# Four tiles instead of six transposed on TensorE, first norms of ten tiles moved behind all statistics, half of w3 loaded in phase one

## The chip, the core and the metric

The kernel runs on one core of one Trainium2 chip. The metric is the device time of one launch in microseconds (us); lower is better. The times before the change are six runs with a median of 1507.94 us (1507.79 to 1508.09). The engines are named as the profile names them: PE is TensorE (matmul), PEld its weight loads, DVE is VectorE, ACT is ScalarE, POOL is GpSimd, SP is SyncE, which here only starts DMA transfers. A trailing q (SPq, POOLq) marks the issuing side of a queue.

## What is computed

The input `x` has 2048 tokens of 1024 bf16 numbers. It is normalized to `xn`; the output is `x` plus a memory-augmented attention over `xn` plus an MLP-mixer block over `xn`. The change lies in the first part of the mixer block:

```python
xn = layernorm(x)
# mixer block, with x := xn
h  = gelu(layernorm(xn) @ w1)                   # phase one
hs = shifted(h, by quarter of the columns) @ w2 # phase two
x1 = xn + hs
B  = x1 + gelu(layernorm(x1) @ w3) @ w4         # phase three, w3 is 1024 x 3584
out = x + attention(xn) + B
```

Both layer norms of phase one have the same row statistics as source: the second norm of `x` is computed straight from `x` with a scale of its own, so one set of statistics gives the "first norm" (`xn`, needed in phase two and in the attention) and the "second norm" (`xn2`, the operand of the product with w1).

## The kernel before

The 2048 tokens are 16 tiles of 128 rows. Weights are k-major: a tile of 128 rows times 1024 columns is 8 blocks of 128 x 128.

**Phase one.** For tile n, `norm_stats` makes the statistics: two BN statistics instructions on DVE (L266, L269), an aggregation (L270), one small DVE instruction that writes `ab` (L271) and a power on POOL that turns it into the scales `rr` (L273). From tile 8 on POOL also makes a negated product `nm2` (L275). `norm2` writes `xn2`: on DVE for tiles 0 to 7 (L282), on ACT for tiles 8 to 15 (L284). The product with w1 needs `xn2` transposed, in `xn2T`, which holds two tiles. Tiles below `NPE` are transposed by TensorE, eight 128 x 128 products with the identity (L303), and copied out of PSUM by ACT (L304). The others are transposed by one DMA from SP (L286). `norm1` writes `xn` into `xn_keep` (L292, DVE).

`stage1(n0, nt, ...)` (L319) is one pass over w1 for `nt` tiles: eight groups, one for each 128 output columns, of eight matmuls (L324) with 128 x nt moving columns. ACT reads each group out of PSUM with a gelu (L326) into `hTB`. Four PSUM buffers take turns, so a group waits for the gelu of the group four before it. `between` hangs further work behind the gelu of one of the eight groups. Tile 0 has a pass of its own (`stage1_k`), tiles 1, 2 and 3 have one each; tiles 4 and 5, 6 and 7 and so on share a pass with 256 columns. I call the passes by their tiles: pass 3, pass 4+5.

Engines run their instructions in the order in which the program gives them, and this part of the order is written by hand on all engines. `prep(n)` (L386) issues the second norm of tile n, the statistics of tile n+1 and the first norm of tile n-2, four tiles ahead of the pass. Tiles of `x` stand in ten buffers (`xt`), so the load of tile n+10 waits for the first norm of tile n. SP issues its DMAs one by one: loads of `x`, transposes, w2 in two halves (L253), four stores of `xn` to a scratch (L407), then parts of w3 (L210). `load_w3` takes the next part of two k-rows and half the columns, 896 KB; four parts make the left half of w3. In the kernel before, two parts are issued at the end of phase one and one each behind tiles 3 and 7 of phase two (L436). The right half is issued at the start of phase three in two DMAs of 1792 KB (L446).

**Phase two** (L414 to L437): for each tile 16 matmuls of 512 columns (L421), an addition of `xn_keep` and statistics on DVE, a norm on ACT (L433), a DMA transpose from SP into `xn3T` (L434) and a store of `x1` issued by POOL (L435). **Phase three** starts with L550 (w3, left half first) and L576 (w4). The value, attention and output phases follow (L607, L673, L731).

Of the kernel before, what the change touches and what calls it, by code (L numbers as in the profile page):

```python
# [16 lines left out]
F32 = mybir.dt.float32  # L17
# [6 lines left out]
P = 128  # L24
S = 2048
D = 1024
KT = D // P
NT = S // P
# [49 lines left out]
def kernel(  # L78
# [112 lines left out]
    with tc.manual_schedule(engines={mybir.EngineType.PE, mybir.EngineType.SP, mybir.EngineType.Pool}), ExitStack() as actx:  # L191
# [6 lines left out]
        with ExitStack() as bctx:  # L198
# [13 lines left out]
            with ExitStack() as hctx:  # L212
# [7 lines left out]
                with ExitStack() as p0:  # L220
                    big = p0.enter_context(tc.tile_pool(name="p0big", bufs=1))
                    ring = p0.enter_context(tc.tile_pool(name="p0ring", bufs=3))
                    w1_sb = big.tile([P, KT, D], BF16)
                    NPE = 6

                    xts = {}

                    def load_x(n):
                        if n < NT:
                            xts[n] = ring.tile([P, D], BF16, tag="xt", bufs=10, name=f"xt{n}")  # L230
                            if n == 0:
                                nc.scalar.dma_start(xts[n][:, 512:], x_v[:, n, 512:])
                                nc.sync.dma_start(xts[n][:, :512], x_v[:, n, :512])
                            else:
                                (nc.gpsimd if n == 12 else nc.sync).dma_start(xts[n][:], x_v[:, n, :])

                    m0 = hTB[:M, 0, 16:16 + D]
                    nc.gpsimd.dma_start(m0, A_mem0[0])
# [18 lines left out]
                    def norm_stats(n, part=None):  # L257

                        if n >= NT:
                            return  # L260
                        xt = xts[n]
                        if n not in stats:
                            stats[n] = [ring.tile(shape, F32, tag=tag, bufs=6, name=f"{tag}{n}") for tag, shape in (("st", [P, 2, 6]), ("mv", [P, 2]), ("ab", [P, 2]), ("rr", [P, 2]), ("nm2", [P, 1]))]
                        st, mv, ab, rr, nm2 = stats[n]
                        if part in (None, 0):
                            nc.vector.bn_stats(st[:, 0, :], xt[:, 0:512])  # L266
                        if part == 0:
                            return
                        nc.vector.bn_stats(st[:, 1, :], xt[:, 512:1024])  # L269
                        nc.vector.bn_aggr(mv[:], st[:])  # L270
                        nc.vector.scalar_tensor_tensor(ab[:], epsm[:], mv[:, 1:2], epsa[:], op0=ALU.mult, op1=ALU.add)  # L271
                        for c in (slice(1, 2), slice(0, 1)) if n == 0 else (slice(0, 2),):
                            nc.gpsimd.tensor_tensor(rr[:, c], ab[:, c], neghalf[:, c], op=ALU.pow)  # L273
                        if n >= 8:
                            nc.gpsimd.tensor_scalar(nm2[:], mv[:, 0:1], rr[:, 1:2], -1.0, op0=ALU.mult, op1=ALU.mult)  # L275
# [13 lines left out]
                    def norm1(n):  # L289
                        st, mv, ab, rr, nm2 = stats[n]  # L290
                        xn = xn_keep[n // 4][:, n % 4]
                        nc.vector.tensor_scalar(xn, xts[n][:], mv[:, 0:1], rr[:, 0:1], op0=ALU.subtract, op1=ALU.mult)  # L292
                        if n < 3:
                            load_x(n + 10)
                        return xn

                    def transposes(xn2, xn2T, jj, half, halves=False):
# [21 lines left out]
                    def stage1(n0, nt, xn2T, between, j0=0):  # L319
                        w = nt * P  # L320
                        for co in range(KT):
                            ps = psum.tile([P, 512], F32, tag="mm", bufs=4)
                            for k in range(KT):
                                nc.tensor.matmul(ps[:, :w].rearrange("p (n t) -> p n t", t=P), w1_sb[:, k, co * P:(co + 1) * P],  # L324
                                                 xn2T[:, j0:j0 + nt, k, :], start=(k == 0), stop=(k == KT - 1))
                            nc.scalar.activation(hTB[:, co, 2 + n0 * P:2 + n0 * P + w], ps[:, :w], ACTF.Gelu_apprx_tanh)  # L326
                            for f in between.get(co, ()):
                                f()
# [20 lines left out]
                    def tr(n, half, halves=False):  # L349
                        transposes(xn2s[n], tiles2[n - n % 2], n % 2, half, halves)  # L350
# [12 lines left out]
                    nc.gpsimd.memset(hTB[:, :, S + 2:S + 4], 0.0)  # L363
                    load_consts(4)
                    nc.gpsimd.memset(sums[:], 1.0)
                    for n in range(1, 6):
                        if n > 1:
                            norm_stats(n + 1, 0)
                        norm2_of(n)
                        norm_stats(n + 1, 1 if n > 1 else None)  # L370
                        if n > 1:
                            norm1(n - 2)
                        if n == 1:
                            stage1_k(tiles2[0])
                        elif n < 4:
                            stage1(n - 1, 1, tiles2[(n - 1) // 2 * 2], {6 - n: [lambda n=n: tr(n, 0)], 7 - n: [lambda n=n: tr(n, 1)]}, (n - 1) % 2)

                    def ahead(n):
                        norm_stats(n + 1, 0)
                        norm2_of(n)  # L380
                        norm_stats(n + 1, 1)
                        if n == 6:
                            norm1(n - 2)

                    stage1(3, 1, tiles2[2], {0: [lambda: tr(4, 0)], 2: [lambda: tr(4, 1), lambda: ahead(6)], 4: [lambda: tr(5, 0)], 5: [lambda: tr(5, 1), lambda: ahead(7)]}, 1)
                    def prep(n):  # L386
                        norm2_of(n)
                        norm_stats(n + 1)
                        if n == 8:
                            norm1(n - 3)  # L390
                        norm1(n - 2)

                    for n0 in range(4, NT, 2):
                        between = {c: [] for c in range(KT)}
                        if n0 + 4 < NT:
                            between[1 + 2 * (n0 == 4)] += [lambda n0=n0: prep(n0 + 4)]
                            between[4 + 2 * (n0 == 4)] += [lambda n0=n0: prep(n0 + 5)]
                        stage1(n0, 2, tiles2[n0], between)
                        if n0 == 4:
                            for n in range(13, NT):  # L400
                                load_x(n)
                        elif n0 in (6, 10):
                            load_w2(n0 // 10)
                    for n in (NT - 2, NT - 1):
                        norm1(n)
                    for i in range(4):
                        nc.sync.dma_start(xn_v[:, 4 * i:4 * i + 4, :], xn_keep[i][:])  # L407
                    for i in range(2):
# [3 lines left out]
                with ExitStack() as p2:  # L412
                    ring = p2.enter_context(tc.tile_pool(name="p2ring", bufs=4))
                    for n in range(NT):  # L414
                        x1 = ring.tile([P, D], F32, tag="x1")
                        st = ring.tile([P, 2, 6], F32, tag="st")
                        for ch in range(2):
                            ps = psum.tile([P, 512], F32, tag="mm", bufs=4)
                            for k in range(KT):
                                o = 2 + n * P + SH[k]  # L420
                                nc.tensor.matmul(ps[:], hTB[:, k, o:o + P], w2_sb[:, k, ch * 512:(ch + 1) * 512], start=(k == 0), stop=(k == KT - 1))  # L421
                            nc.vector.tensor_tensor(x1[:, ch * 512:(ch + 1) * 512], ps[:], xn_keep[n // 4][:, n % 4, ch * 512:(ch + 1) * 512], op=ALU.add)
                            nc.vector.bn_stats(st[:, ch, :], x1[:, ch * 512:(ch + 1) * 512])
                        mv = ring.tile([P, 2], F32, tag="mv")
                        nc.vector.bn_aggr(mv[:], st[:])
                        a = ring.tile([P, 1], F32, tag="a")
                        nc.vector.tensor_scalar(a[:], mv[:, 1:2], EPS, None, op0=ALU.add)
                        r3 = ring.tile([P, 1], F32, tag="r3")
                        nc.gpsimd.tensor_tensor(r3[:], a[:], neghalf[:, 0:1], op=ALU.pow)
                        nm3 = ring.tile([P, 1], F32, tag="nm3")  # L430
                        nc.gpsimd.tensor_scalar(nm3[:], mv[:, 0:1], r3[:], -1.0, op0=ALU.mult, op1=ALU.mult)
                        xn3 = ring.tile([P, D], BF16, tag="xn3")
                        nc.scalar.activation(xn3[:], x1[:], ACTF.Identity, bias=nm3[:], scale=r3[:])  # L433
                        nc.sync.dma_start_transpose(xn3T[n // 4][:, n % 4], xn3[:])  # L434
                        nc.gpsimd.dma_start(R1_v[:, n, :], x1[:])  # L435
                        if n in (3, 7):  # L436
                            load_w3()  # L437

            with ExitStack() as p3:
                psum3 = p3.enter_context(tc.tile_pool(name="psum3", bufs=2, space=PSUM))  # L440
# [593 lines left out]
```

## Time and profile before

| what | value |
|---|---|
| median of six runs | 1507.94 us |
| the profiled execution's own time | 1507.74 us |
| its span in the profile | 1506.0 us |
| granted TensorE clock, all stages | 1.00 |
| phase one on PE (first pass to last gelu group) | 7.46 to 66.4 us |
| phase two on PE | 66.4 to 121.7 us |
| PE busy in 24.21 to 66.40 us | 42.12 of 42.19 us |
| PE busy in 66.40 to 121.70 us | 54.98 of 55.30 us |
| DMA busy share, 31 to 67 us / 67 to 121 us | 0.87 / 1.03 |
| DVE busy share, 24 to 31 us / 67 to 121 us | 6.79 of 7.0 us / 46.9 of 54 us |

The rows of the table are the answers of the profile for single stretches of time. "Busy" of PE includes overlapping ends of pipelined matmuls: a matmul row says 219 ns for 128 columns, while the starts of neighbouring ones lie 56 ns apart. For costs on PE the distance of the starts counts, not the row's length. Some matmul records are missing (49 of 50 in each stretch of phase two), which looks like a gap of 0.2 us and is none. The trace also keeps for each DMA the time at which its completion is signalled; "lands" in this text is that time.

### The profile page before, as it was taken

The numbers are of one execution on the slowest core, as the hardware profiler recorded it, in microseconds if no ns is written. First come the engines' busy times: TensorE is split into PE (matmuls) and PEld (weight loads), VectorE is DVE, ScalarE is ACT, GpSimd is POOL, SyncE is SP. The second block draws the span as 40 slices with busy tenths as digits, with TensorE's granted clock in tenths as the row PEclk, the third lists the DMA queues.
The fourth block names the chain that finished last, engine by engine and source line by source line (L and its number), as shares of the span: only waits on it lengthen the run. The fifth ranks groups of instructions, "written<-read, shape, count | busy, mean of one in ns | idle before, by whom it ended". The sixth has DMA issues, their size and how long they took to land.

```text
span 1506.0 us, 24219 instructions
## 1 busy us (share of the span) xinstructions
PE 1496.4 (99%) x9757; PEld 803.2 (53%) x9828; DVE 546.7 (36%) x1148; ACT 501.8 (33%) x1140; POOL 166.2 (11%) x234
## 2 busy tenths in 40 slices
PE   9999999999999999999999999999999999999999
PEld 8744444445454444444466645664665455545555
DVE  8382330100110112221146624651564166516642
ACT  6433103013012011111256614650663266406630
POOL 4141020211211221100000010001000100010001
PEclk9999999999999999999999999999999999999999
DMA  7999762353455777622389956992997299918921
GB/s 191 277 266 327 214 178 89 134 202 113 154 161 139 193 239 253 209 98 84 126 226 252 244 125 174 255 233 78 240 253 203 72 229 225 214 63 204 212 49 51
DMA packets 306194, 272.89 MB, mean 181 GB/s; under 512 B 155766, under 2 KB 272280, under 8 KB 306080
## 3 DMA queue, kind: packets, MB, share of 16 engines
q1 hardware_dynamic: 284704, 193.18, 51.5%
q0 software_dynamic: 20544, 76.89, 15.0%
q8 instruction: 79, 1.29, 0.4%
q10 hardware_dynamic: 832, 1.25, 0.3%
q14 instruction: 35, 0.29, 0.1%
HBM read 190.05 MB, written 45.29 MB: 156 GB/s over the span
## 4 chain that ended last, share of the span: by engine, by line
PE 99%; DVE 0%; issue 0%; DMA 0%; ACT 0%; POOL 0%; ACTq 0%
PE ps L673 30%; PE ps L607 15%; PE pso L731 15%; PE ps L550 13%; PE ps L576 13%; PE ps L421 4%; PE ps L324 3%; PE psS L688 2%; PE psO L712 2%; PE ps L871 1%; PE ps L502 1%; PE ps L471 0%; PE gps L485 0%; PE ps L314 0%; PE ps L303 0%
## 5 line engine op out<-in xcount | busy, mean ns | idle before, releaser
L673 PE MATMUL ps<-hTb,wt 128*128 128x396 bf16 (+2 forms) x2528 | 484.8, 342 | 0.0
L673 PEld LDWEIGHTS <-wt 128*128 128x128 bf16 x2528 | 236.8, 98 | 175.4
L607 PE MATMUL ps<-wt,xT 128*128 128x512 bf16 x1004 | 220.1, 379 | 1.1
L731 PE MATMUL pso<-wo_sb,oX 128*128 128x512 bf16 (+1 forms) x972 | 208.3, 372 | 1.1
L550 PE MATMUL ps<-xn3T,w_sb 128*128 128x512 bf16 x896 | 196.2, 379 | 0.0
L576 PE MATMUL ps<-w_sb,h3T 128*128 128x512 bf16 x873 | 194.1, 379 | 1.2
L607 PEld LDWEIGHTS <-xT 128*128 128x128 bf16 x1024 | 100.2, 98 | 120.8
L551 ACT ACTIVATE h3T<-ps 128x512 bf16<-128x512 f32 x112 | 66.8, 597 | 290.7 <-PE ps L550 289.8
L731 PEld LDWEIGHTS <-oX 128*128 128x128 bf16 x992 | 96.3, 98 | 107.6
L675 ACT CAST KT<-ps 128x462 bf16<-128x462 f32 (+2 forms) x160 | 81.7, 510 | 203.3 <-PE ps L673 199.1
L576 PEld LDWEIGHTS <-h3T 128*128 128x128 bf16 x896 | 87.1, 98 | 103.6
L550 PEld LDWEIGHTS <-w_sb 128*128 128x128 bf16 x896 | 86.7, 98 | 102.2
L694 DVE TENSOR_REDUCE sums<-sm 99x4 f32<-99x396 f32 (+2 forms) x176 | 97.6, 555 | 114.0 <-ACT sm L692 114.0
L677 ACT ACTIVATE QT<-ps 128x462 bf16<-128x462 f32 (+2 forms) x160 | 83.8, 524 | 120.6 <-PE ps L673 106.3
L609 ACT CAST Vs<-ps 128x512 bf16<-128x512 f32 x64 | 37.5, 586 | 232.2 <-PE ps L607 223.6
L690 DVE TENSOR_TENSOR sm<-psS,c_mask_reg_sb 99x396 f32<-99x396 f32 x152 | 86.7, 570 | 72.8 <-PE psS L688 72.6
L613 DVE CAST Vs<-ps 128x512 bf16<-128x512 f32 x64 | 44.3, 692 | 171.6 <-PE ps L607 166.1
L692 ACT ACTIVATE sm<-sm 99x396 f32<-99x396 f32 (+2 forms) x176 | 92.7, 527 | 34.2 <-DVE sm L690 27.6
L700 DVE TENSOR_TENSOR Pn<-sm,rs 99x396 bf16<-99x396 f32 (+2 forms) x176 | 98.9, 562 | 6.6 <-DMA PT<-Pn 0.7
L738 POOL DMA_DIRECT2D out_dram<-ot x30 | 16.4, 545 | 697.7 <-DVE ot L737 697.6
L577 DVE TENSOR_TENSOR R<-ps,R 128x512 f32<-128x512 f32 x32 | 22.0, 690 | 181.1 <-PE ps L576 172.0
L737 DVE TENSOR_TENSOR ot<-pso,Rt 128x512 bf16<-128x512 f32 (+1 forms) x33 | 22.2, 675 | 166.8 <-PE pso L731 162.6
(130 smaller groups left out, 1038.3 us busy)
## 6 DMA issues: line engine op xcount, KB each, us to landing
wt<-in_A_Wq_dram SPq DMA_DIRECT2D x76, 512.0 KB
wt<-in_A_Wk_dram SPq DMA_DIRECT2D x76, 512.0 KB
wt<-in_A_Wv_dram POOLq DMA_DIRECT2D x24, 1024.0 KB, 6.6
V_scratch<-Vs SPq DMA_DIRECT2D x32, 512.0 KB
V<-V_scratch SPq DMA_DIRECT2D x40, 384.0 KB
w_sb<-in_B_w_dram SPq DMA_DIRECT2D x9, 1024.0 KB
R_scratch<-x POOLq DMA_DIRECT2D x16, 512.0 KB, 4.4
R<-R_scratch SPq DMA_DIRECT2D x16, 512.0 KB
```

The source lines that it names most:

```text
L550: nc.tensor.matmul(ps[:].rearrange("p (n t) -> p n t", t=P), w3_sb[:, k, f * P:(f + 1) * P], xn3T[tb][:, :, k, :], start=(k == 0), stop=(k ...
L551: nc.scalar.activation(h3T[:, f, :], ps[:], ACTF.Gelu_apprx_tanh)
L576: nc.tensor.matmul(ps[:], h3T[:, f, j * P:(j + 1) * P], w4_sb[:, f, ch * 512:(ch + 1) * 512], start=(f == 0), stop=(f == FT - 1))
L607: nc.tensor.matmul(ps[:], xT[:, m4 * 4 + j, k, :], wv[:, k, :], start=(k == 0), stop=(k == KT - 1))
L673: nc.tensor.matmul(ps[:, :nb], w[:, k, hh * P:(hh + 1) * P], B["hT"][:, k, :nb], start=(k == 0), stop=(k == KT - 1))
L675: nc.scalar.copy(dst[:, hh, :], ps[:, :nb])
L677: nc.scalar.mul(dst[:, hh, :], ps[:, :nb], scale)
L690: nc.vector.tensor_tensor(sm[:T, :, :T], S3, t["mask"][:].unsqueeze(1).to_broadcast((T, 4, T)), op=ALU.add)
L692: nc.scalar.activation(e[:T, :, :T], sm[:T, :, :T], ACTF.Exp, scale=LN2)
L694: nc.vector.tensor_reduce(ss, e[:T, :, :T], axis=AX.X, op=ALU.add)
L700: nc.vector.tensor_tensor(Pn[:T, :, :T], e[:T, :, :T], rs[:T, :].unsqueeze(2).to_broadcast((T, 4, T)), op=ALU.mult)
L731: nc.tensor.matmul(self.ps[:, :self.w], self.oX[0][:, h, self.oX[1] + self.gl * P:self.oX[1] + (self.gl + 1) * P], wo_sb[:, h, self.cc], s ...
```

## The change

Six edits, all in phases one and two:

1. `NPE` goes from 6 to 4: tiles 4 and 5 are transposed by DMA. Pass 4+5 becomes two passes, 4 and 5, of 128 columns each.
2. Second norms and statistics of tiles 4 to 7 are all issued on DVE before pass 3, and pass 3 has nothing hung between its groups.
3. First norms: of tiles 0 and 1 they are issued behind the second norms of tiles 4 and 5, of tiles 2 to 5 in `prep(9)` to `prep(12)`, of tiles 6 to 15 behind the statistics of tile 15. `mv` and `rr` get ten buffers, `st`, `ab` and `nm2` four (all had six).
4. Loads of `x`: tiles 10 and 11 go from SP's queue to POOL's; tiles 13, 14 and 15 follow the first norms of tiles 3, 4 and 5 one at a time, no longer together behind pass 4+5.
5. `prep(8)` to `prep(15)` hang elsewhere: `prep(8)` behind group 5 of pass 5; 9, 10, 11 behind groups 0, 3, 6 of pass 6+7; 12, 13 behind groups 2, 5 of pass 8+9; 14, 15 behind groups 2, 5 of pass 10+11. The first half of w2 is issued behind pass 8+9, not 6+7.
6. Two parts of w3 are issued on SP right behind the transpose of tile 7, the other two stay behind the stores of `xn`. Phase two loads none.

On every engine the instructions behind phase two stand in the same order in both kernels.

```diff
-                    NPE = 6
+                    NPE = 4
...
-                                (nc.gpsimd if n == 12 else nc.sync).dma_start(xts[n][:], x_v[:, n, :])
+                                (nc.gpsimd if n in (10, 11, 12) else nc.sync).dma_start(xts[n][:], x_v[:, n, :])
...
-                            stats[n] = [ring.tile(shape, F32, tag=tag, bufs=6, ...
+                            stats[n] = [ring.tile(shape, F32, tag=tag, bufs=10 if tag in ("mv", "rr") else 4, ...
...
-                        if n < 3:
-                            load_x(n + 10)
+                        load_x(n + 10)
...
-                    for n in range(1, 6):
+                    for n in range(1, 4):
...
-                        if n > 1:
-                            norm1(n - 2)
...
+                    for n in range(4, 8):
                         norm_stats(n + 1, 0)
                         norm2_of(n)
                         norm_stats(n + 1, 1)
-                        if n == 6:
-                            norm1(n - 2)
-
-                    stage1(3, 1, tiles2[2], {0: [lambda: tr(4, 0)], 2: [lambda: tr(4, 1), lambda: ahead(6)], 4: [lambda: tr(5, 0)], 5: [lambda: tr(5, 1), lambda: ahead(7)]}, 1)
+                        if n < 6:
+                            norm1(n - 4)
+                    for i in range(2):
+                        load_w3()
+                    stage1(3, 1, tiles2[2], {}, 1)
+                    firsts = list(range(2, NT))
+
                     def prep(n):
                         norm2_of(n)
                         norm_stats(n + 1)
-                        if n == 8:
-                            norm1(n - 3)
-                        norm1(n - 2)
-
-                    for n0 in range(4, NT, 2):
-                        between = {c: [] for c in range(KT)}
-                        if n0 + 4 < NT:
-                            between[1 + 2 * (n0 == 4)] += [lambda n0=n0: prep(n0 + 4)]
-                            between[4 + 2 * (n0 == 4)] += [lambda n0=n0: prep(n0 + 5)]
+                        if 8 < n < 13:
+                            norm1(firsts.pop(0))
+
+                    stage1(4, 1, tiles2[4], {}, 0)
+                    stage1(5, 1, tiles2[4], {5: [lambda: prep(8)]}, 1)
+                    for n0 in range(6, NT, 2):
+                        at = {6: ((9, 0), (10, 3), (11, 6)), 8: ((12, 2), (13, 5)), 10: ((14, 2), (15, 5))}.get(n0, ())
+                        between = {c: [lambda n=n: prep(n)] for n, c in at}
                         stage1(n0, 2, tiles2[n0], between)
-                        if n0 == 4:
-                            for n in range(13, NT):
-                                load_x(n)
-                        elif n0 in (6, 10):
+                        if n0 in (8, 10):
                             load_w2(n0 // 10)
-                    for n in (NT - 2, NT - 1):
-                        norm1(n)
+                    while firsts:
+                        norm1(firsts.pop(0))
...
-                        if n in (3, 7):
-                            load_w3()
```

More of the change, by code (lines that the diff above doesn't have):

```diff
@@ L262, in norm_stats @@
                         if n not in stats:
-                            stats[n] = [ring.tile(shape, F32, tag=tag, bufs=6, name=f"{tag}{n}") for tag, shape in (("st", [P, 2, 6]), ("mv", [P, 2]), ("ab", [P, 2]), ("rr", [P, 2]), ("nm2", [P, 1]))]
+                            stats[n] = [ring.tile(shape, F32, tag=tag, bufs=10 if tag in ("mv", "rr") else 4, name=f"{tag}{n}") for tag, shape in (("st", [P, 2, 6]), ("mv", [P, 2]), ("ab", [P, 2]), ("rr", [P, 2]), ("nm2", [P, 1]))]
                         st, mv, ab, rr, nm2 = stats[n]
@@ L370 @@
                         norm_stats(n + 1, 1 if n > 1 else None)
-                        if n > 1:
-                            norm1(n - 2)
                         if n == 1:
                             stage1_k(tiles2[0])
-                        elif n < 4:
+                        else:
                             stage1(n - 1, 1, tiles2[(n - 1) // 2 * 2], {6 - n: [lambda n=n: tr(n, 0)], 7 - n: [lambda n=n: tr(n, 1)]}, (n - 1) % 2)
-                    def ahead(n):
+                    for n in range(4, 8):
                         norm_stats(n + 1, 0)
```

## The prediction

> **What bounds the kernel now.** I read the busy shares and the chain of waits on the page first, to see which engine sets the end.
>
> ```profile
> PE 1496.4 (99%) x9757; PEld 803.2 (53%) x9828; DVE 546.7 (36%) x1148; ACT 501.8 (33%) x1140; POOL 166.2 (11%) x234
> PE 99%; DVE 0%; issue 0%; DMA 0%; ACT 0%; POOL 0%; ACTq 0%
> ```
>
> PE works for 1496.4 of 1506.0 us: everything else can give back 9.6 us at most, in all stages together. So the question is what the change does to PE's own work, and whether it makes PE wait. Next the timeline of PE around passes 3 and 4+5, for the price of the work that is removed (columns: start, length, engine, line, operation, count).
>
> ```profile
> 20.19 0.39 PE L303 MATMUL ps<-ident,xn 128*128 128x128 bf16 x4
> 20.41 1.06 PE L324 MATMUL ps<-xn2T,w_sb 128*128 128x128 bf16 x16
> 21.31 0.39 PE L303 MATMUL ps<-ident,xn 128*128 128x128 bf16 x4
> ```
>
> Each row starts where the one before has issued its last matmul: 4 transposes take 20.41 - 20.19 = 0.22 us, 16 matmuls of 128 columns 0.90 us, both 56 ns apiece (55.8 in the records). In passes of 256 columns the starts lie 109.2 ns apart. Looking for larger distances between starts, I find only one real one from 11 us to the end of phase two: 0.347 us before 31.44, 0.24 too much, between passes 4+5 and 6+7. The chain of that stretch names it.
>
> ```profile
> 29.88 0.67 ACT xn L284
> 30.55 0.47 issue
> 31.02 0.37 ACT hTB L326
> 31.39 0.04 issue
> 31.44 0.60 PE ps L324 x4
> ```
>
> ACT had idled 1.59 us for the statistics of tile 8, then ran its second norm (1.24 us); the gelu behind it freed a PSUM buffer too late. Last, the transposes on SP, and the w3 load nearest to the one that is moved.
>
> ```profile
> 24.36 1.36 SPq L286 DMA_TRANSPOSE xn2T<-xn  x1
> ...
> 31.14 3.18 SPq L286 DMA_TRANSPOSE xn2T<-xn  x2
> ...
> 127.47 1.17 SPq L210 DMA_DIRECT2D w_sb<-in_B_w_dram  x2
> ```
>
> By the records of completions the transpose issued at 24.36 (tile 6) lands at 29.71, that of tile 7 (issued 27.01) at 30.50, tiles 8 and 9 (31.14, 33.08) at 34.20 and 36.13: 3.06 us alone, 5.35 at worst. Of the two 1792 KB loads issued from 127.47 the first lands at 135.33: 7.86 us.
>
> **PE's work.** Sixteen transposes go: 16 x 55.8 ns = -0.89 us. Pass 4+5 becomes two passes: 2 x 64 x 55.8 = 7.14 us for 64 x 109.2 = 6.99, +0.16. Both are on PE, hence on the path. ACT loses four copies (L304, 0.585 us each) and reads 16 groups of 128 columns (0.28 us) for 8 of 256 (0.38): less work, covered as before.
>
> **The stall at 31.44.** `prep(8)` now hangs behind group 5 of pass 5. Pass 3 starts at 19.75 as before and takes 3.57 us, so pass 4 starts at 23.32, pass 5 at 26.89, pass 6+7 at 30.46. Group 5 ends at 29.57, its gelu near 30.0. Tile 8's scales were ready at 29.3 and come no later without the first norm at 25.31 ahead of them. ACT then runs 1.24 us and the two gelus behind it end by 31.8; their buffers are wanted at 32.2 and 33.1. No wait: -0.24 us.
>
> **Transposes on the DMA.** DVE's chain for a tile is `ab`, the power on POOL, second norm, statistics. In the before rows the second norm of tile 4 starts at 18.35, 0.04 after POOL's 0.92 us power. The first norms that ran beside that chain at 14.54 and 17.23 are gone, and without one the power took 0.69: tile 4 is issued at 18.5 to 18.9, tile 5 by 21.6, tile 6 at 23.9 to 24.4, tile 7 at 26.3 to 27.0. With 3.06 us tile 4 lands by 22.0, ahead of 23.32; with 5.35 at 24.3, a stall of 1.0. Tile 5 has until 26.89. Tiles 6 and 7, with the latencies that these two had, land by 29.7 and 30.5, just in time for 30.46. I take no stall, since the queue is empty around 19 to 22 (0.26 busy in that stretch), and keep 1.0 for the range. Here the Trainium skill speaks against the change: "VectorE: DVE Perf Modes", section "The three transpose paths", puts a 128x128 block at 390 ns on TensorE and 1309 on the DMA, and its rules prefer TensorE when PSUM will do. By its figure eight blocks need an estimated 10.5 us, tile 4 lands near 29.2 and PE waits 5.9: slower by 5 us at the least. By the rows here a whole tile lands in 3.06 to 5.35, and on a core that PE bounds the block's 56 ns on PE are what counts. I go by the rows.
>
> **w3 ahead of tiles 8 and 9.** On SP the two parts (1.83 MB) follow the transpose of tile 7, so they are issued near 27.9, and the transposes of tiles 8 and 9 queue behind them. Pass 8+9 starts at 30.46 + 6.99 = 37.45. ACT issues the norm of tile 8 at 30.0 and of tile 9 behind group 0 of pass 6+7, near 32.1; tile 9 reaches SP at 33.3 and alone would land at 36.4. With the row's 7.86 us for the same bytes on a queue as empty, w3 lands at 35.8. Tile 12, which stood behind a w2 half in the same way, landed 0.97 us after it, tile 13 another 0.92 later: tiles 8 and 9 at 36.7 and 37.6. That is a stall of 0.2 us, where the cover is used up. The skill's "DMA: Bandwidth & Descriptors", section "Anatomy of one DMA", fits 2.0 us plus bytes over 436 GB/s (for POOL's queue): estimated 6.2 us, tile 9 at its own 36.4, no stall, a sum of -0.97. I take the row: +0.2. The ends are 0 and, at the pace of a single part in phase two (below), 8.
>
> **What else moves, at no cost.** POOL gets two issues (0.75 us in its row for tile 12), tile 10 near 21 and tile 11 near 23.7, between powers that DVE asks for every 2.7 us; behind them waits only the next power, at 22.8 and 25.5. Landed 3.2 us later, both precede their statistics near 29. Tiles 13 to 15 are loaded one at a time behind the transposes of 10 to 12, near 37, 39.7 and 43; with the 3.0 us of their row and 1.8 of statistics tile 13 is ready at 42 to 44 for ACT's slot at 43.1, and an ACT that waits 1 us is covered by PSUM buffers worth 2.6. The transposes of 13 and 15 are wanted at 51.4 and 58.4 and land by 49 and 56.5. The ten late first norms take DVE 0.46 us each: from 48 to 53, and phase two adds them only from 66. The stores of xn keep their place, 53.4, behind the second half of w2, which landed at 60.2 and still does.
>
> **Phase two** loses two 896 KB loads while its DMA share is 1.03. That looks like the gain, but PE's starts show no wait in phase two, and the first w3 columns were there long before 121.7. What becomes faster, the transposes into `xn3T`, waits for nobody: 0. The right half of w3, issued behind the last of them, keeps its time, as does all that follows.
>
> **Sum.** -0.89 + 0.16 - 0.24 + 0.2 = -0.77 us. The profiled execution took 1507.74 us (span 1506.0 and 1.74 around it), 0.20 below the median of the runs: 1506.97 for it, **1507.2** on the runs' median.
>
> **Rivals.** *Small stalls eat the gain.* For it: four deadlines (tiles 4, 6/7, 9) with margins under 1.3 us, and tile 6's 5.35. Stalls don't add, since PE's delay moves the later deadlines. A whole stall of 1.0 at tile 4, or 1 to 2.5 at tile 9, gives 1507.9 to 1509.5. Against: the median latency is near 3.5. *w3 blocks the queue (the slow side).* In phase two a part issued at 85.89 landed at 92.03, one issued at 99.85 at 106.47, 6.1 and 6.6 us for 896 KB each, and the transposes behind them 2.3 us apart. Two in a row at that pace land at 40.6, tile 9 at 45.2, PE waits 7.8 us: 1507.94 - 0.97 + 7.8 = 1514.8. It decides "slower" once tile 9 lands behind 41.4. Against: stores of x1 shared the engines there, and only tile 12's load does here. *The freed DMA of phase two pays*, a gain of 3 us or more: nothing in PE's starts for it. *It doesn't do what it says*: a transpose that still waits on an early first norm; the order on DVE excludes it.
>
> **How the numbers follow.** A measurement of this kernel tells about 0.2% (3.0 us) from no change. The forecast (own range 1506.8 to 1507.9) has 0.66, small stalls 0.24, blocking by w3 or DMA transposes at the skill's price 0.08, a large gain 0.02. The first two lie within 0.2%: same 0.90, slower 0.08, faster 0.02. The range, 1506.7 to 1509.2, takes in most of the small stalls and leaves the rest out.
>
> **What would show it.** Starts of L324 56 ns apart from 19.75 to 30.5, then 109; L303 with 32 products for 48; no start distance over 0.2 us at 23.3, 26.9 and 30.5; 0.1 to 0.3 at 37.5. Tile 9's landing against 37.5 decides between forecast and rival; a PE stall of several us there makes me wrong, and so does any change of length behind 66 us.

## The result, and the profile after

The changed kernel takes **1510.28 us** (median of 18 runs, 1508.9 to 1518.47) where the kernel before takes 1508.06 in the same comparison (39 runs): a ratio of 1.0018, 95% interval 1.001 to 1.0026. The forecast was 1507.2 with a range up to 1509.2, so the change costs 2.2 us where a gain of 0.8 was foretold. The profiled execution of the changed kernel took 1510.99 us (span 1509.2), 3.2 us more span than before.

The page's first and fourth parts (busy time and share, then the chain by engine):

```profile
span 1509.2 us, 24329 instructions
PE 1498.3 (99%) x9805; PEld 804.5 (53%) x9876; DVE 546.5 (36%) x1148; ACT 501.6 (33%) x1144; POOL 166.5 (11%) x236
...
PE 99%; DMA 1%; issue 0%; SPq 0%; DVE 0%
```

PE is busy 1.9 us *longer* though sixteen transposes left it, and the DMA now has 1% in the chain. Both signs are needed: a pure wait would have raised the span but not PE's busy time. The place of the wait is in PE's waits between 11 us and the end of phase one, where the kernel before had none on a DMA (engine, line: total, times, longest):

```profile
PE ps L323 <- DMA xn2T<-xn: 2.1, 1, 2.1
```

One wait, for one transpose. The chain from 30 to 45 us says which one and when (start, length, what):

```profile
29.98 0.78 PE ps L323 x14
30.76 0.13 issue
30.89 2.61 PE ps L323 x23
33.50 6.50 DMA xn2T<-xn
39.99 0.14 issue
40.13 4.88 PE ps L323 x28
```

The transpose issued at 33.50 is that of tile 9. It lands at 39.99, and pass 8+9 starts behind it; PE had been ready at 37.87, so the pass starts 2.26 us late (the waits count it without the issue at its end). The second sign is in the windows behind that wait (columns: PE, PEld, DVE, ACT, POOL busy with counts, then granted clock, DMA share, GB/s):

```profile
37.90:40.10 2.20, 0.14 (x2) 0.00 (x1) 0.92 (x2) 1.08 (x2) 0.00 (x0) 1.00 0.75 159
...
41.00:44.40 3.40, 3.40 (x18) 2.34 (x16) 2.63 (x7) 0.77 (x2) 1.53 (x3) 0.50 0.74 207
```

In the second of them PE is never idle, yet the clock is 0.50 and only 18 matmuls fit into 3.40 us. The clock's records put it at half from 41.00 to 44.41, 3.413 us. In that stretch sixteen matmuls of 256 columns started 213 ns apart, not 109: 16 x 104 = 1.67 us.

Laid side by side from the starts of the passes, in us:

| stretch | before | after | difference | foretold |
|---|---|---|---|---|
| start of pass 3 | 19.75 | 19.88 | +0.13 | 0 |
| passes 3, 4 and 5 | 11.45 | 10.72 | -0.73 | -0.73 |
| wait ahead of pass 6+7 | 0.24 | 0.29 | +0.05 | -0.24 |
| wait ahead of pass 8+9 | 0 | 2.26 | +2.26 | +0.2 |
| half clock in pass 8+9 | 0 | 1.67 | +1.67 | 0 |
| start of phase two | 66.37 | 69.74 | +3.37 | -0.77 |
| from there to the end | 1439.64 | 1439.46 | -0.17 | 0 |

All of the loss but the 0.13 lies between 30 and 45 us. Phase two, which lost two 896 KB loads, and all that follows are as long as before. The runs differ in one line of this table: of 20 executions of the changed kernel, the timed ones and two more, ten report a mean granted clock of 1.000 and ten less. The ten have a median of 1509.36; the seven at 0.999, which is what 3.4 us of half clock make in 1509, have 1511.14. The difference, 1.78, is the table's 1.67. So a run that keeps its clock is 1.3 us above before (the three lines above it in the table make 1.58), and half of the runs pay the clock on top; the median falls between. Three more are at 0.997 and 0.998 and reach 1518.47, more than their clock explains (0.002 x 1517 us is 3.0); what else delays them is not known. The kernel before has single runs of that size as well (1514.30 in the same comparison, 1515.18 in a later one), so such a tail need not come from the change.

Why is tile 9 late? The queue of SP, which issues the transposes and most loads (start, length, operation, count):

```profile
18.43 9.70 SPq L286 DMA_TRANSPOSE xn2T<-xn  x4
28.18 1.09 SPq L210 DMA_DIRECT2D w_sb<-in_B_w_dram  x2
31.33 7.62 SPq L286 DMA_TRANSPOSE xn2T<-xn  x3
39.00 0.57 SPq L235 DMA_DIRECT2D xt<-in_A_x_dram  x1
```

The two w3 parts go at 28.18 and 28.81 and have landed at 36.02, 7.84 us behind the first issue. Tile 8, issued at 31.33, lands at 36.92. Tile 9, issued at 33.50, lands 3.07 us behind tile 8, not 0.92. Three things could hold it. The first is the w3 bytes ahead of it. The second is tile 12 of x. POOL issues it in both kernels, but it waits for the first norm of tile 2, which the change moved into `prep(9)`; so it now falls between the issues of tiles 8 and 9, and lands at 39.16. POOL's row before, then after:

```profile
20.95 0.75 POOL L235 DMA_DIRECT2D xt<-in_A_x_dram  x1
...
32.34 0.62 POOL L235 DMA_DIRECT2D xt<-in_A_x_dram  x1 [0.20 <-issue]
```

The third is a packet of another kind. The DMA's own view from 36.3 to 40.2 us (40 slices of 0.0975 us, busy share in tenths, each packet counted whole where it starts; then the queues):

```profile
DMA  6994090999999200020001000909999999999999
...
q8 instruction: 1, 0.02, 1.8%
```

From 37.5 to 38.7 almost no packet starts, in the midst of tile 9's transpose, and 21 packets of the transpose that start near 37.45 last 1.3 to 1.5 us. The one packet of the instruction queue is a 16 KB block of PE's instructions; it starts at 36.54 and takes 1.10 us. In the kernel before, this fetch came at 40.7. It fell on the transpose of tile 11, which took 5.2 us to land at 42.74 and wasn't wanted before 45.4. By the time of the fetch the changed kernel has sent PE 96 more instructions, 64 products and their weight loads from splitting pass 4+5, less 16 transposes and theirs, so the fetch comes 4 us earlier. The Trainium skill's "Runtime: NRT & Kernel Launch", section "Instruction fetch mechanics", has the block (256 instructions through a DMA queue of the sequencer's own) and calls its cost mostly hidden; here it is hidden from PE's issue, but perhaps not from a transpose beside it.

### The profile page after: what moved, and what is told of

Read it like the earlier page. It is cut to its first block, busy times and chain, and to the rows that moved or that the text cites. A ratio compares the mean times of both kernels' runs of the same rounds, so it can differ in the third digit from the quotient of the medians.

```text
span 1509.2 us, 24329 instructions
## 1 busy us (share of the span) xinstructions
PE 1498.3 (99%) x9805; PEld 804.5 (53%) x9876; DVE 546.5 (36%) x1148; ACT 501.6 (33%) x1144; POOL 166.5 (11%) x236
## 4 chain that ended last, share of the span: by engine, by line
PE 99%; DMA 1%; issue 0%; SPq 0%; DVE 0%
PE ps L666 30%; PE ps L600 15%; PE pso L724 15%; PE ps L543 13%; PE ps L569 13%; PE ps L416 4%; PE ps L323 3%; PE psS L681 2%; PE psO L705 2%; PE ps L864 1%; PE ps L495 1%; PE gps L478 0%; PE ps L464 0%; DMA w_sb<-in_B_w_dram 0%; DMA xn2T<-xn 0%
```

## The experiments

The theories that the expectations weigh are these three causes and the clock. "Wanted" is when PE is ready for pass 8+9. A kernel that differs from another by one edit is named after it. The kernels ran in three comparisons, in which the kernel before took 1508.10 us (the first four), 1508.16 and 1507.88. A time is the span plus 1.7 to 2.4 us around it, and in the medians this part differs by up to half a microsecond among the kernels (1.77 before, 2.23 where it is shifted by 92 instructions), so smaller differences of medians say nothing.

### w3 back in phase two, and w3 alone on the kernel before

The first kernel undoes only the w3 part of the change; the second does only that part.

```diff
--- changed kernel
-                    for i in range(2):
-                        load_w3()
                     stage1(3, 1, tiles2[2], {}, 1)
...
+                        if n in (3, 7):
+                            load_w3()
```

> The changed kernel with the two early w3 parts taken back into phase two (behind tiles 3 and 7), all else as changed. Theory w3: the two parts stand ahead of tiles 8 and 9 on SP's queue and cause the whole loss; without them tile 9 lands near 36.5, pass 8+9 starts without a wait, no half clock at 41 to 44.4; -0.73 on PE and about the same 0.2 to 0.3 us wait at pass 6+7 leave 0.7 us less than before: ratio 0.9995, about 1507.3. Rival (the other edits: x loads on POOL's queue, the moved norms): tile 9 still lands behind 39, PE still waits about 2 us, ratio near 1.0015.

> The kernel before with one edit: two w3 parts issued behind the transpose of tile 7, none in phase two. Theory w3: tile 9 lands near 38 to 40, while pass 8+9 wants it at 38.4; PE waits 0 to 2 us, and if it waits about 2 us a window of half clock follows: ratio 1.000 to 1.0025. Rival (other edits): no wait, ratio 1.0000.

Without early w3 the changed kernel takes 1508.72 (13 runs, 1507.59 to 1509.79), ratio 0.9998 (0.9989 to 1.0007). A loss against before can no longer be told from nothing, though the median is 0.6 above, and PE still waits in the profiled execution:

```profile
PE ps L323 <- DMA xn2T<-xn: 1.5, 1, 1.5
```

Tile 9, issued at 33.42, took 5.86 us to 39.27 with no w3 ahead of it. The instruction fetch fell at 35.9, and the transpose's packets of that moment last 1.9 to 2.4 us. Four runs lie at 1507.6 to 1507.9 and nine at 1508.5 to 1509.8, so the wait seems not to come in every run.

On the kernel before, early w3 costs nothing: 1507.87 (13 runs), ratio 0.9999 (0.999 to 1.0007). Its chain from 30 to 45 us is PE's passes alone, with no DMA in it. w3 lands 8.0 us behind its issue there, tile 8 0.87 behind w3 and tile 9 another 0.86 later, at 38.21, wanted at 38.3. This is the queue as the prediction had it (7.86, 0.97 and 0.92). So the w3 loads alone use up the margin and no more, and without them something else suffices to miss the deadline.

### The wait filled with work

Ten matmuls of 512 columns on zeros ahead of pass 8+9, into a PSUM tile that nothing reads, keep PE busy until tile 9 has landed.

```diff
--- changed kernel
+                        if n0 == 8:
+                            pf = psum0.tile([P, 4, P], F32, tag="tr", name="fill")
+                            for i in range(10):
+                                nc.tensor.matmul(..., wz[:, :P], wz[:], start=(i == 0), stop=(i == 9))
                         stage1(n0, 2, tiles2[n0], between)
```

> The changed kernel with ten matmuls of 512 columns on zeros ahead of pass 8+9, 2.16 us of work whose result is not used. Theory clock: PE's wait of 2.26 us is what brings the window of half clock (3.41 us, 1.7 us lost); with the wait filled the granted clock stays 1.00 from 31 to 67 and the time falls 1.5 us below the changed kernel's, to about 1508.7, with a narrower spread. Rival (the half clock comes from elsewhere): the window of half clock stays and the time is as changed or up to 2 us longer.

Windows from the filled wait on, columns as above:

```profile
38.00:40.10 2.10, 2.05 (x10) 0.81 (x9) 0.88 (x2) 1.05 (x2) 0.00 (x0) 1.00 0.88 160
...
41.00:44.40 3.40, 3.40 (x33) 3.04 (x32) 2.40 (x7) 2.18 (x4) 1.26 (x3) 1.00 0.88 209
```

Tile 9 lands as late as before (40.04), but the clock stays at 1.00, and 33 matmuls fit where there were 18. Phase two starts at 68.12, not 69.74, and the profiled span is 1507.5: the gap in PE's work made the half clock. The median fell less than the full price, to 1509.75 (16 runs, ratio 1.0013, 1.0005 to 1.002), since it can only fall by what half of the runs paid: here 15 of 16 runs have a clock of 1.000, and ten of 20 did before. Its median lies 0.4 above that of the ten (1509.36).

### The fetch moved off tile 9

PE's program begins with twelve matmuls on zeros that warm the clock. Cut into more and narrower ones with about as many columns, they add instructions ahead of the fetch and move it forward in time.

```diff
--- changed kernel
-                    for i in range(12):
-                        nc.tensor.matmul(ps[:], wz[:, :P], wz[:], ...)
+                    for i in range(48):
+                        nc.tensor.matmul(ps[:, :P], wz[:, :P], wz[:, :P], ...)
```

> The changed kernel with PE's warm-up as 48 matmuls of 128 columns, not 12 of 512: the same streaming time ahead of the first tile, 72 more PE instructions, so that PE's 16 KB instruction fetches come 2 to 4 us earlier and no longer at 36.55. Theory fetch: the standstill of tile 9's transpose (packets from 37.45 last 1.3 us) comes from the fetch beside it; without it tile 9 lands near 37.7 to 38.5, PE waits 0 to 0.7 us, no half clock, time 1507.3 to 1508. Rival (the queue alone): tile 9 still lands near 40, time near 1510.

With 72 more instructions the fetch comes at 34.0 instead of 36.5, so its place does follow the count. There w3 is still under way, and tile 8's transpose with it; packets of that transpose from 34.2 to 35.3 last up to 1.9 us. Tile 9 lands at 38.87, PE waits 1.42, and the median is 1509.7 (21 runs, ratio 1.0015, 1.0008 to 1.0021). The run alone can't decide on the fetch, which may have been moved from one transpose onto another. (The kernel with 92 instructions, next, answers that: with the fetch at 33.0 packets of tile 8 still last up to 1.5 us, and tiles 8 and 9 land within 0.06 us of the same times. So at 34.0 the fetch cost nothing that can be told.)

So the next pair uses 58 matmuls of 106 columns (92 more instructions), once on the changed kernel and once on the one with w3 back in phase two.

> The changed kernel, both w3 parts early, with the same 58 x 106 warm-up, the fetch near 31. Theory fetch: tiles 8 and 9 follow w3 at 0.9 us each as in before_w3_early, tile 9 lands at 37.5 to 38, PE waits 0 to 0.5 us, no half clock: near 1507.5 (0.9996). Theory x12: tile 12's load still stands between them, tile 9 lands at 38.5 to 39, wait 1 to 1.5 us: 1508.5 to 1509.5.

> w3_as_before with PE's warm-up as 58 matmuls of 106 columns, not 12 of 512: the same streaming, 92 more PE instructions, so that the 16 KB instruction fetch seen at 35.92 comes near 31, between the transposes of tiles 7 and 8. Theory fetch: that fetch beside tile 9's transpose is what makes it stand still; tile 9 lands by 37, pass 8+9 starts without a wait, time near 1507.3 (ratio 0.9995), spread under 1 us. Theory x12 (tile 12's load from POOL's queue, issued at 32.35 between the transposes of 8 and 9, is what delays it): tile 9 still lands near 39, wait 1.5 us, time 1508.5 or more.

Without early w3 the wait is gone: tile 9 lands at 36.86, 2.4 us ahead of its landing without the shift, the fetch is at 29.9, and the chain from 30 to 45 us is one piece.

```profile
29.97 15.08 PE ps L323 x144
```

The median is 1507.59 (13 runs; ratio 1.0, 0.9992 to 1.0008), 1.1 below the kernel without the shift. Phase two starts 57.84 us after the first pass, where it was 58.90 in the kernel before: 1.06 less, for 0.97 that the prediction's sum gives without its term for w3. With early w3 the fetch falls at 33.0, w3 lands at 36.40 and tile 8 0.90 behind it, but tile 9 1.51 later still: tile 12's load landed at 38.05 in between. PE waits 1.52, median 1509.34 (22 runs, ratio 1.0013, 1.0006 to 1.0019). So w3 and tile 12 together are enough without a fetch on tile 8 or 9. The chain of this run shows a second way by which a late transpose reaches PE:

```profile
31.18 6.12 DMA xn2T<-xn
...
37.40 1.24 ACT xn L284
38.64 0.28 ACT hTB L325
...
38.95 6.06 PE ps L323 x54
```

The 6.12 us are tile *8*. Three buffers serve `xn2`, so ACT's norm of tile 11 waits until tile 8 is out of its own; the gelu behind that norm frees PSUM for PE at 38.92. Tile 9, landed at 38.81, would have released PE at 38.95 as well. Two waits end together, and removing one alone would gain nothing.

### Tile 12 loaded at the start

Tile 12 goes into a part of `xn_keep` that is free until the end of phase one, from SP's queue at the start, and POOL no longer loads it. Done with and without early w3, and with early w3 and the 92 instructions.

```diff
--- changed kernel
...
+                            if n == 12:
+                                xts[n] = xn_keep[3][:, 0]
+                                nc.sync.dma_start(xts[n][:], x_v[:, n, :])
+                                return
...
-                    for n in range(7, 10):
+                    for n in (7, 8, 9, 12):
                         load_x(n)
```

> The changed kernel with tile 12 of x loaded at the start as in x12_early_w3_as_before. Theory x12: tile 9 lands near 37.7 behind w3 and tile 8, PE waits 0.2 us, near 1507.4 (0.9996). Theory fetch: the fetch at 36.5 stops tile 8 or 9 for 1.3 us, tile 9 lands near 39, wait 1 to 1.5 us, 1508.5 to 1509.5 (1.0006).

> w3_as_before with tile 12 of x loaded on SP at the start (behind tile 9, straight into its place in xn_keep) and no load on POOL near 32; PE's instructions and so its fetches as in w3_as_before. Theory fetch: the fetch near 36 still stops tile 9's transpose, unless that is over by then because nothing is in its way: lands near 37 to 38.5. Theory x12: tile 9 lands 3.1 us after its issue, near 36.5, ahead of the fetch or not, no wait, near 1507.3 (0.9995).

> The changed kernel, both w3 parts early, with both other suspects taken away: tile 12 loaded at the start and the 58 x 106 warm-up that moves the fetch off tiles 8 and 9. Theory of three parts: w3 alone leaves tile 9 where the queue puts it, 0.9 us behind tile 8 and 1.8 behind w3, landing 37.5 to 38.0; PE waits 0 to 0.5 us, no half clock, median near 1507.5 to 1508.0 (ratio 0.9997 to 1.0000). Rival (w3 with this order is itself enough for the loss): wait over 1 us, 1508.8 or more.

With w3 in phase two and tile 12 early the wait of 1.62 is gone (tile 9 at 36.87, median 1508.12, 13 runs, ratio 0.9999, 0.9991 to 1.0007); but its fetch also moved, to 34.1, between the two transposes, so this run doesn't separate tile 12 from the fetch. (Its profiled execution, the slowest of the 13, waits 1.3 us for a load of weights at the start of phase three.) With early w3 and tile 12 early, 1509.15 (13 runs, ratio 1.0006, 0.9998 to 1.0014). Tile 9 is still late, landing at 38.77 for a wait of 1.19, but now it stands only 0.72 behind tile 8; it is tile 8 that comes 2.5 us after w3 (35.56 to 38.05), with the fetch at 35.8 on it. With the fetch moved to 33.4 as well, only w3 is left. The chain of that kernel from 30 to 45 us:

```profile
29.97 3.62 PE ps L329 x44
33.59 4.74 DMA xn2T<-xn
38.33 0.14 issue
38.47 6.60 PE ps L329 x59
```

w3 lands at 36.49, tile 8 0.89 and tile 9 another 0.95 later, at 38.33, and PE waits 0.50 (median 1508.11, 13 runs, ratio 1.0001, 0.9993 to 1.0009). The prediction had written down a landing at 37.6 and a stall of 0.2; the spacing is its own, and w3 landed 0.7 us later than it assumed.

### The fetch put onto tile 9, all else as before

The runs so far move a fetch together with other things. The last pair adds it alone: the kernel before with early w3, whose margin is used up but not exceeded, gets 80 more instructions (52 warming matmuls of 118 columns), so that its fetch falls from 41.4 to 37.7, onto tile 9.

> before_w3_early, which lost nothing, with a warm-up of 52 x 118 columns: 80 more PE instructions move its fetch from 41.4 to near 37, onto tile 9's transpose. Theory fetch: the transpose stands still beside the fetch, tile 9 lands 1 to 1.7 us later than 38.2, PE waits 1 to 1.5 us ahead of pass 8+9 (wanted at 38.3), in some runs with a window of half clock: median 1509 or more (1.0006 or more), with a tail. Rival (the fetch is innocent, the loss in the changed kernel comes from its other edits): no wait, 1507.9, as before_w3_early.

Tile 8 lands at 37.60, within 0.25 us of its place without the fetch. Tile 9 follows at 40.01, 2.4 us later where it was 0.86. The chain from 30 to 45 us, then the DMA's view from 37 to 40.2 (40 slices of 0.08 us):

```profile
29.90 2.60 PE ps L324 x24
32.49 7.51 DMA xn2T<-xn
40.01 0.14 issue
40.14 4.96 PE ps L324 x44
```

```profile
DMA  9999999999997030399970010200100399099999
...
q8 instruction: 1, 0.02, 2.0%
```

A standstill as in the changed kernel, from 38.7 to 39.5, and PE waits 1.78. The kernel without the fetch on its transpose shows a short dip between 37.9 and 38.1 and no standstill (36 to 38.4, slices of 0.06 us):

```profile
DMA  7241999999999999999999999999999582179999
```

The median is 1510.12 (13 runs, 1509.23 to 1511.09), 2.25 above the same kernel without the 80 instructions, in another comparison, and every run lies above all 13 of that kernel. Not all of it is tile 9: in the profiled execution 1.8 us arise here, and PE waits 1.0 us (0.2 without the 80) for a transpose in the attention phase, near 798. The later fetches have moved as well. Its ratio to the kernel before, 1.0008 (0.9998 to 1.0018), doesn't exclude 1, since that comparison has a wider spread. The delay of tile 9 is the fetch's, and shown as such: the only edit cuts the warm-up at the very start of PE's program into 40 more matmuls on zeros, and the transpose is late where the fetch now falls. All 13 runs have a clock of 1.000, so this wait of 1.78 didn't bring the half clock.

The records of single packets suggest how one fetch holds all the rest. The fetch ends at 38.77. From there to 39.57 the trace has a chain of packets that run one at a time, first ten small ones of the transpose, then some of the x loads behind it. The 19 packets that had started before the chain last 0.9 to 1.3 us, and all end when it does, between 39.55 and 39.65. So it looks as if one engine, held up by the fetch, works off its share while the others wait for it; the records don't name the engine. In the changed kernel the chain starts with three packets of tile 12 (0.44, 0.36 and 0.17 us, from 37.63, where its fetch ends), which is how the two causes come to act together there. The kernel before has the same picture at tile 6: a fetch from 25.52 to 27.07, a chain from there to 27.8, and 19 packets of the transpose that last 1.4 to 1.7 us.

### A version with all three undone

Of the change this keeps the four tiles on TensorE, the late first norms and the separate passes; w3 stays in phase two, tile 12 is loaded at the start and the warming matmuls are 58 of 106 columns.

> x12_early_w3_as_before with the 58 x 106 warm-up: the two passes of 128 columns, w3 as in the kernel before, tile 12 loaded at the start, the fetch near 31. All theories: no wait at pass 6+7 or 8+9, -0.73 on PE and the 0.24 of the old stall gained: about 1507.1, ratio 0.9993, at the edge of what five rounds tell from 1. A wait at pass 8+9 would speak against the part of x12 and of the fetch both.

It takes 1507.47 (13 runs, 1507.11 to 1510.85) where the kernel before takes 1507.88 in the same comparison; ratio 0.9998 (0.9989 to 1.0006). Phase two starts 58.42 us after the first pass, where it was 58.90. The chain from 30 to 45 us is PE alone, and no wait is left ahead of passes 6+7 and 8+9. The 0.4 us (0.6 by the medians of the spans, 1505.5 for 1506.1) are of the size of what the table's second line gains, but the interval doesn't tell them from nothing.

What each run has ahead of pass 8+9, and what PE waits there in the profiled execution (us):

| kernel | w3 early | tile 12 on POOL near 32 | fetch | tile 9 lands | PE waits |
|---|---|---|---|---|---|
| changed | yes | yes | 36.5, on tile 9 | 39.99 | 2.26 |
| shifted by 72 | yes | yes | 34.0, w3 under way | 38.87 | 1.42 |
| shifted by 92 | yes | yes | 33.0, w3 under way | 38.81 | 1.52 |
| tile 12 early | yes | no | 35.8, on tile 8 | 38.77 | 1.19 |
| tile 12 early, shifted | yes | no | 33.4, w3 under way | 38.33 | 0.50 |
| w3 in phase two | no | yes | 35.9, on tile 9 | 39.27 | 1.62 |
| w3 in phase two, shifted | no | yes | 29.9, before both | 36.86 | 0 |
| w3 in phase two, tile 12 early | no | no | 34.1, between 8 and 9 | 36.87 | 0 |
| before, early w3 | yes | no | 41.4, behind both | 38.21 | 0 |
| before, early w3, fetch moved | yes | no | 37.7, on tile 9 | 40.01 | 1.78 |

Early w3 lets tile 9 land 1.5 to 2.1 us later (38.33 for 36.87, 38.81 for 36.86, and 38.21 for the 36.13 of the kernel before), tile 12 on POOL 0.5 more beside it (38.81 for 38.33), the fetch 1.2 to 2.4 (39.99 for 38.81; 40.01 for 38.21; 39.27 for 36.86). They don't add simply, and the wait at the head of pass 8+9 begins where tile 9 lands behind about 38.

## Why the prediction was wrong

**PE's work** was right: sixteen transposes less and one pass split gave -0.73, as the sum had it. The changed kernel's row in PE's timeline, in the place of the three of before, has 128-column products and nothing else for 12 us:

```profile
19.32 12.06 PE L323 MATMUL ps<-xn2T,w_sb 128*128 128x128 bf16 x205
```

**The stall at 31.44** was right in its cause and not in its gain. ACT's norm of tile 8 ran at 30.08 (foretold 30.0), and the gelu was not late. But the 0.24 us were taken by what was next in line: tile 7's transpose, issued at 26.30, landed at 30.75 (foretold: by 30.5, "just in time for 30.46"), and PE started at 30.89. The prediction had written the two times down 0.04 apart and counted the difference as zero; it had no term for the 0.14 us between landing and start either.

**Transposes on the DMA.** The skill's price, 10.5 us for a tile, was off the mark, as the prediction took it: tile 4 was issued at 18.43 and landed at 21.58, 3.15 us, and tile 6 took 6.0 at worst, with a fetch on it at 26.66. The 5.35 us that the prediction read as the worst latency had a fetch on it as well, the one at 25.52; so the trace of the kernel before already held the cause that the sum leaves out. No wait at tiles 4 and 5.

**w3 ahead of tiles 8 and 9** is where it failed. Its terms for w3 (7.86 us, measured 7.84) and for tile 8 (36.7, measured 36.92) held. The term that failed is "tiles 8 and 9 at 36.7 and 37.6", that is, tile 9 0.92 behind tile 8, taken from the transposes of tiles 12 and 13, which followed each other on one queue with nothing between. Measured: 3.07. Two things stood between that the sum had not counted: the load of tile 12, which the prediction names in a rival ("only tile 12's load does here") and gives no time on the DMA, and a fetch of PE's instructions, whose place moves with the 96 instructions that the splitting adds. With w3 alone tile 9 is 0.95 behind tile 8, with tile 12 as well 1.51, with the fetch on it 3.07. The fetch is shown by the last pair; tile 12 by "shifted by 92" with and without it. With both out of the way the spacing was as forecast, and the wait 0.50 us.

**The price of a wait** was the second failure. The sum priced an idle PE at its length. In half of the executions the clock fell below full speed, which cost 1.67 us behind the 2.26 us of idleness in the profiled one; the filled run shows that the idleness brings it. The Trainium skill's "TensorE: Matmul & The Clock Gate", section "What's actually happening", has half clock after an idle window of some 3.4 us and calls that window free-running, and "HAM oscillation — how this bites in real kernels" names idle gaps above about 3.4 us as what to avoid. The measured length of half clock, 3.413 us, is that window's; the gap that brought it was shorter, 2.26 us, and waits of 1.78 and 1.62 brought none in 13 runs each, while of the two kernels with 1.42 and 1.52 four of 21 and five of 22 runs report less than 1.000.

The clock's records show what counts. Up to the last, their stretches are whole multiples of 3.413 us (34.133 us, ten of them, ahead of the half clock; 1501.864, or 440, in the kernel before), and they begin at another time in each trace: 4.37 us before, 6.86 in the changed kernel, 5.74 in the last pair's. So I count windows of 3.413 us on from there and take PE's idle time in each. A matmul counts as busy to the end of its row, which makes the gap of 2.26 one of 2.09. In the changed kernel a window runs from 37.58 to 41.00 and holds the whole gap; the half clock follows at its end. In the last pair's trace a window ends at 39.87, inside the gap of 1.78, and holds 1.35 of it; no half clock follows. Over all 13 traces, with the last windows, where PE runs out of work, each of the 14 windows with 2.08 us or more of idleness is followed by half clock, and no window with 1.99 or less is. So what counts is the idle time inside one window, and here some 2.0 of its 3.4 us are enough. A gap of 2.09 us at a random place has at least 2.04 in one window in an estimated 0.4 of the cases (all but 1.99 of 3.41), which fits ten of 20; the runs without a trace can't show it.

**The rest** held: nothing in phase two, DVE's late norms covered, the stores and the second half of w3 unmoved (-0.17 us behind 66 us). The rival "small stalls eat the gain" had the place and the wait, "1 to 2.5 at tile 9", and ended at 1509.5 for want of the clock. "w3 blocks the queue" was wrong in its mechanism: w3 landed at 36.02, not 40.6. The range ended where the first rival did.

What stays open: whether the other DMA engines do wait for the one that the fetch holds, as the packets suggest in five traces of the experiments and at tile 6 of the kernel before; why the wait of the kernel without early w3 spares some runs, and the runs of the changed kernel above 1514.

## What to carry to other kernels

A margin of a few tenths on a DMA transpose is no margin: list everything that lies on the DMA engines in those microseconds, other engines' queues and the instruction fetches too, and ask what moves them. On a core that PE bounds, price a wait of PE near two microseconds with the half clock that may follow it, and don't expect a load moved off a stage to pay where PE never waited for it. A count of instructions early in the program is a way to move a fetch off a transpose, but look where it lands.

## What the runs showed of the hardware

- A 16 KB fetch of PE's instructions beside a DMA transpose delays the transpose: with 80 more PE instructions tile 9 landed at 40.01 and not at 38.21. In the changed kernel the fetch itself took 1.10 us.
- One gap of 2.26 us in PE's work gave 3.413 us of half clock in the profiled execution, and ten of 20 executions report a mean clock below 1.000. Gaps of 1.2 to 1.8 us gave none in their profiled executions, but nine of 43 runs of two of these kernels report less than 1.000. The price per window, 1.67 us by the starts of the matmuls, is 1.78 by the medians of the runs at 1.000 and at 0.999.
- The clock changes at the edges of windows of 3.413 us, whose phase differs from trace to trace (the first edge on record at 4.37, 5.74 and 6.86 us). In 13 traces half clock follows every window in which PE is idle for 2.08 us or more, and none with 1.99 or less.
